# The second matrix product of an attention and MLP kernel, computed for eight of nine blocks with seven half-size products in place of eight

## The chip, the cores and the metric

The kernel runs on one core of a Trainium2 chip. The core has a matrix engine (PE, TensorE; its weight loads are shown apart as PEld), two engines for elementwise work that can read the matrix engine's result memory (DVE, VectorE, and ACT, ScalarE), a third elementwise engine that works between tiles in SBUF alone in this kernel and also issues part of the DMAs (POOL, GpSimd), and an engine that only issues DMAs here (SP, SyncE). Matrix results land in PSUM, which this kernel treats as one tile `pb` of 8 banks of 512 fp32 columns on 128 partitions. The metric is device time of one execution in microseconds; lower is better.

## The reference

Eight batches, eight heads, 576 positions, head size 64. A bias that depends on the distance of two positions alone is added to the scores, and the attention result is the input x (4608 rows by 512) of an MLP:

```python
scores = scale * np.matmul(q, k.transpose(0, 1, 3, 2)) + bias   # bias by distance
attn = softmax(scores)
x = (attn @ v).transpose(0, 2, 1, 3).reshape(4608, 512)
h = x @ w_in                                # 4608 x 2048
g = h + sin(alpha * h) ** 2 / (alpha + 1e-09)
out = g @ w_out                             # 4608 x 512
```

## The kernel before

All matrix operands are fp16, all sums fp32. The MLP's rows are cut into nine blocks of 512 (0 to 8); the attention is done batch by batch, t = 0 to 7. One turn t has two stages. In the *attention stage* PE multiplies k and q for 21 units (16 of kind "A", and C, B and X units for the last 64 positions), each into one or two of the PSUM banks 0 to 5; ACT takes the exponential of each unit into a tile `u`; DVE multiplies by the bias factor (L738, two SBUF operands `u` and `m2r`); PE multiplies by v (`plan_av`), DVE divides by the sums (L952, L953) into `xn`, and a transposing DMA issued on SP writes the result into `xT`. In the *MLP stage* `plan_moe_in` computes block b = t: for each of 16 slices f of 128 hidden columns, four matmuls of `w_in` and `xT` into one bank, sine on ACT (L1068), square on ACT or DVE (L1075, L1077), and DVE writes slice f of the tile `g` (L1082). ACT changes its function table between the stages. Turn 7 does blocks 7 and 8.

The product that is changed is `plan_mo(b, a)`: for each 128 rows a = 0 to 3 of block b, 16 matmuls of 128 x 512 (one for each f; weights are the slice of g, the moving operand is row block f of `w_out`) accumulate in one bank. The tag "mo" may use banks 7 and 6 and so may the attention times v ("av"); in practice one holds a tile of the one and one a tile of the other. DVE or ACT copies the finished bank to `outs` and SP stores it.

The order of all work is not written by hand. `Plan.run` is a list scheduler that runs when the program is built: each piece of work is a `Task` with a cost for every engine that can do it, dependencies, a priority and buffers; the plan emits tasks in the order of its own clock, and each engine's queue then has that fixed order. On the chip an engine takes its queue strictly in order and waits at semaphores that the framework sets for every hazard on a tile. The `plan_mo` matmuls have the lowest priority and are marked `fill`: they go between the other PE work, at most `QUOTA` = 44 of them during an attention stage. So block b's w_out product runs on PE mostly during the attention stage of turn b + 1, and in the tail after turn 7 for blocks 7 and 8.

Three things of the plan matter below. First, work that is emitted inside another task is not costed: when slice 0 of g is written, `gg` also emits, on POOL, a one-element copy that waits for that slice (`tick`), six loads of v and two DMAs that stage k and q for turn b + 2:

```python
if f == 0 and 1 <= b < T - 1:
    nc.gpsimd.tensor_copy(out=tick, in_=gcell[b].v[0:1, 0, 0:1])
    load_v16(b + 1)
    if b + 2 < T:
        stage_kq(b + 2)
```

Second, on SP the loads of the next turn's k and q (`load_kqT`, L396 and L397) stand behind the transposing DMAs of this turn, and POOL's two copies of k's last 64 rows (L402) wait for them and stand ahead of `tick` in POOL's queue. Third, a framework semaphore orders two engines' accesses to the same PSUM bank by the order in which they were emitted.

## Time and profile before

| what | value |
|---|---|
| median of 3 timed runs | 373.82 us (372.97 to 376.73) |
| span of the profiled execution | 374.9 us |
| PE busy | 368.2 us |
| ACT busy | 315.7 us |
| DVE busy | 257.8 us |
| POOL busy | 91.9 us |
| matmuls of g and w_out, 128 x 512 | 560, and 16 each of 384 and 128 columns |

The page of the profile gives no time of the profiled execution besides its span, which runs from the first to the last instruction; it lies 0.3% above the median and within the three runs. "Busy" of PE counts a matmul from start to its modelled end; matmuls are pipelined, so the duration of one (0.379 us for 512 columns) is longer than the step from one start to the next. A line of the timeline merges instructions of one kind that follow each other: start, length of the whole stretch, engine, line, operation, tiles, shape and count, and in brackets the idle time before it and what ended it.

### The profile page before, as it was taken

What the parts mean: (1) busy time and instruction counts of PE and PEld (TensorE: products, weight loads), DVE (VectorE), ACT (ScalarE), POOL (GpSimd) and SP (SyncE); (2) the same over time, 40 slices, a digit from 0 to 9 for tenths busy, and PEclk for the clock granted to TensorE, in tenths of its full rate; (3) what the DMA queues carried; (4) which work ended last, traced back from release to release, by engine and by line L of the source; (5) the groups of instructions that cost most, each with busy time, mean ns of one, the idle gap of its engine ahead of it and who ended that gap; (6) DMA issues with size and microseconds to landing.
All of it is one profiled execution on the core that took longest, in us unless ns stands there. A gap on an engine that the chain in (4) does not pass through costs nothing.

```text
span 374.9 us, 8925 instructions
## 1 busy us (share of the span) xinstructions
PE 368.2 (98%) x3576; PEld 197.4 (53%) x3576; DVE 257.8 (69%) x559; ACT 315.7 (84%) x431; POOL 91.9 (25%) x133
## 2 busy tenths in 40 slices
PE   8999999999999999999999999999999999999996
PEld 3455454644455455684564455444576455444443
DVE  3496976759676967597758867786759675879000
ACT  2787989979997999899989999799979997999211
POOL 7368270037000640055002800090006000000000
PEclk9999999999999999999999999999999999999999
DMA  9969999369922998199917992699249121000112
GB/s 168 201 113 192 200 173 160 83 112 112 133 64 62 151 143 123 48 160 137 133 48 134 125 168 58 122 88 187 59 111 118 65 58 47 7 27 5 73 69 85
DMA packets 149114, 40.49 MB, mean 108 GB/s; under 512 B 137080, under 2 KB 143568, under 8 KB 149072
## 3 DMA queue, kind: packets, MB, share of 16 engines
q0 software_dynamic: 96032, 17.67, 58.3%
q1 hardware_dynamic: 52864, 22.16, 24.6%
q8 instruction: 28, 0.46, 0.5%
q10 hardware_dynamic: 176, 0.09, 0.1%
q14 instruction: 14, 0.11, 0.1%
HBM read 37.73 MB, written 16.56 MB: 145 GB/s over the span
## 4 chain that ended last, share of the span: by engine, by line
PE 95%; ACT 3%; DVE 1%; issue 0%; ACTq 0%
PE pb L457 92%; ACT u L707 3%; PE pb L556 2%; PE pb L1024 1%; PE pb L550 0%; DVE xn L953 0%; DVE u L738 0%; DVE qT L539 0%; DVE zz L508 0%; ACT outs L537 0%; ACT xT L537 0%; DVE rd L952 0%; PE pb L646 0%; PE pb L934 0%; ACTq L537 0%
## 5 line engine op out<-in xcount | busy, mean ns | idle before, releaser
L707 ACT ACTIVATE u<-pb 128x1024 f16<-128x1024 f32 (+1 forms) x146 | 137.4, 1017 | 11.9 <-PE pb L457 10.5
L457 PE MATMUL pb<-w_out,g 128*128 128x512 f16 (+2 forms) x592 | 139.0, 374 | 0.0
L457 PE MATMUL pb<-xT,w_in 128*128 128x512 f16 (+4 forms) x704 | 127.4, 340 | 0.0
L1082 DVE SCALAR_TENSOR_TENSOR g<-sq,inv_a,pb 128x512 f16<-128x512 f16 x144 | 101.3, 744 | 7.1 <-PE pb L457 2.7
L1068 ACT ACTIVATE s<-pb,alphaT 128x512 f16<-128x512 f32 x144 | 92.9, 692 | 12.4 <-PE pb L457 11.9
L457 PEld LDWEIGHTS <-w_in 128*128 128x128 f16 x704 | 64.6, 98 | 57.4
L457 PEld LDWEIGHTS <-g 128*128 128x128 f16 x592 | 53.9, 98 | 60.2 <-issue 5.6
L738 DVE TENSOR_TENSOR u<-u,m2r 128x512 f16<-128x512 f16 (+1 forms) x128 | 62.3, 493 | 33.6 <-ACT u L707 31.9
L457 PEld LDWEIGHTS <-u 128*128 128x128 f16 x1152 | 43.4, 97 | 9.6 <-issue 4.6
L402 POOL COPY kt<-kT 64x256 f16<-64x256 f16 x12 | 4.9, 410 | 172.0 <-DMA kT<-staged_k 107.8
L457 PE MATMUL pb<-qT,kT 64*128 64x64 f16 (+1 forms) x512 | 43.3, 293 | 1.1 <-ACT u L707 0.6
L1075 ACT ACTIVATE sq<-s 128x512 f16<-128x512 f16 x69 | 43.1, 637 | 1.2 <-DVE g L1082 0.3
L457 PE MATMUL pb<-v,u 128*128 128x65 f16 x1024 | 43.7, 193 | 0.0
L1077 DVE TENSOR_TENSOR sq<-s 128x512 f16<-128x512 f16 x75 | 30.9, 422 | 12.5 <-ACT s L1068 11.7
L953 DVE TENSOR_TENSOR xn<-pb,rd 128x256 f16<-128x256 f32 (+2 forms) x59 | 28.5, 483 | 2.0
L457 PEld LDWEIGHTS <-kT 64*128 64x128 f16 x512 | 16.2, 95 | 23.1 <-issue 16.8
L457 PE MATMUL pb<-vh,u 128*128 128x130 f16 x128 | 28.2, 221 | 0.0
L407 POOL DMA_DIRECT2D v<-in_v_dram x28 | 24.8, 900 | 4.0 <-DMA nat<-in_k_dram 2.1
L537 ACT ACTIVATE outs<-pb 128x512 f32<-128x512 f32 (+2 forms) x12 | 6.9, 572 | 19.9 <-PE pb L457 19.9
L952 DVE RECIPROCAL rd<-pb 128x4 f32<-128x4 f32 (+2 forms) x59 | 11.0, 186 | 13.3 <-PE pb L457 13.1
L539 DVE COPY outs<-pb 128x512 f32<-128x512 f32 x25 | 17.2, 686 | 4.1 <-PE pb L457 4.1
L1146 ACT ACT_TABLE_LOAD x15 | 19.2, 1283 | 0.3
(75 smaller groups left out, 192.5 us busy)
## 6 DMA issues: line engine op xcount, KB each, us to landing
out_dram<-outs SPq DMA_DIRECT2D x35, 256.0 KB, 2.8
v<-in_v_dram POOLq DMA_DIRECT2D x28, 128.0 KB, 4.6
staged_k<-in_k_dram POOLq DMA_DIRECT2D x6, 576.0 KB, 8.9
staged_q<-in_q_dram POOLq DMA_DIRECT2D x6, 576.0 KB, 12.1
w_in<-in_moe_w_in_dram POOLq DMA_DIRECT2D x4, 512.0 KB, 8.5
w_out<-in_moe_w_out_dram POOLq DMA_DIRECT2D x4, 512.0 KB, 14.5
w_out<-in_v_dram SPq DMA_DIRECT2D x6, 128.0 KB, 5.7
xT<-xn SPq DMA_TRANSPOSE x47, 2.4
```

The lines of the kernel that those rows point to most:

```text
L407: nc.gpsimd.dma_start(out=vs[t % 2][:, c, :, 0:D], in_=vp[128 * c : 128 * c + 128],)
L457: nc.tensor.matmul(out=out, lhsT=lhsT, rhs=rhs, start=start, stop=stop)
L539: k_of(e).tensor_copy(out=o, in_=i)
L707: nc.scalar.activation(out=o, in_=x, func=AF.Exp, scale=0.125)
L738: nc.vector.tensor_tensor(out=io, in0=io, in1=m2[:, 2 * p : 2 * p + 2, x0 : x0 + hi - lo], op=ALU.mult)
L952: nc.vector.reciprocal(out=r, in_=x[:, :, :, D])
L953: nc.vector.tensor_tensor(out=xn[:, 0:n].rearrange("p c (z d) -> p c z d", z=2), in0=x[:, :, :, 0:D], in1=r.unsqueeze(3).to_broadcast([128 ...
L1068: nc.scalar.activation(out=s16.v, in_=h.v, func=AF.Sin, scale=alphaT[:, f : f + 1])
L1075: nc.scalar.activation(out=sq.v, in_=s16.v, func=AF.Square)
L1077: k_of(e).tensor_tensor(out=sq.v, in0=s16.v, in1=s16.v, op=ALU.mult)
L1082: nc.vector.scalar_tensor_tensor(out=gcell[b].v[:, f, :], in0=sq.v, scalar=inv_a[:, f : f + 1], in1=h.v, op0=ALU.mult, op1=ALU.add,)
L1146: nc.scalar.preload_act_table_set(name)
```

## The change

Blocks 1 to 8 get `plan_mo_w` in place of `plan_mo`; block 0 is as before. The product of one block, g (512 rows by 2048) times w_out (2048 by 512), is cut into 2 by 2: rows 0 to 255 and 256 to 511 of g, columns 0 to 255 and 256 to 511 of w_out, and even and odd slices f of the sum. Strassen's method in Winograd's form makes the four quarters of the result from seven products instead of eight. The products' operands are quarters of g and w_out or sums of them:

- Sums of w_out, once (`plan_wt`): 12 pieces of 128 x 512 into three new tiles `wt`, and four in place, all on POOL.
- Sums of g, for each block: S1 to S4, each in two pieces of 128 x 1024 (four slices by 256), on DVE or POOL as the plan chooses. S3 and S2 go to new tiles `half3` and `half2`, S1 and S4 overwrite quarters of g. In each piece S1 follows S3 and S2 follows S1; S4 follows S2 and product 2.
- Seven products, each 2 x 8 matmuls of 128 x 256: for rows c = 0 and 1 of 128, eight slices f. They all use bank 7, columns 0 to 255 for c = 0 and 256 to 511 for c = 1, and all blocks 1 to 8 hold that bank as one buffer, "mw", so that "av" keeps bank 6 alone.
- After each product and c, 256 columns are taken out of PSUM: a copy (DVE or ACT) after products 1 and 2, an addition with an earlier fp32 result on DVE (tiles `sn`, `outs`) after the other five. Two products accumulate onto the one before them in PSUM, after its value was taken out.
- The result goes out in quarters of 256 x 256, one DMA for both c.

Around it: blocks 2 to 7 let the first two slices' matmuls of `plan_moe_in` start before all of x is there (`SPLIT`), the attention tail of the turn before goes into the second run of units instead of the first (`TAIL_RUN`), the scheduler's window and one priority are larger, and several small tiles of the start share memory with `wt[0]`. The start flag of the `w_in` matmuls is set once per bank.

```diff
-NBUF = {"ut": 2, "u": 2, "g": 2, "s16": 3, "sq": 3, "outs": 5, "xn": 6}
+NBUF = {"ut": 2, "u": 2, "g": 2, "s16": 3, "sq": 3, "outs": 5, "xn": 6, "s2": 1, "s3": 1, "sn": 3}
-BANKS = {"h": (0, 1, 2, 3, 4, 5), "av": (6, 7), "mo": (7, 6)}
+BANKS = {"h": (0, 1, 2, 3, 4, 5), "av": (6, 7), "mo": (7, 6), "mw": (7,)}
-WINDOW = 700
+WINDOW = 900
+T_WT = 50.0
+SG = 4
+TAIL_RUN = 1
-SPLIT = {0: 3, 1: 3}
+SPLIT = {0: 3, 1: 3, **{b: 2 for b in range(2, 8)}}
-AV_PRI = 400
+AV_PRI = 800
...
+    wt = [sgl.tile([128, 8, 256], F16, name=f"wt{i}") for i in range(3)]
+    half = {k: sgl.tile([128, 8, 256], F16, name=f"half{k}") for k in (2, 3)}
...
-            tl = plan_tail(t - 1, base) if i == 0 and t > 1 else None
+            tl = plan_tail(t - 1, base) if i == TAIL_RUN and t > 1 else None
...
+    def plan_wt():
+        w = w_out16.rearrange("p (f z) n -> p z f n", z=2)
...
+            x1 = sub(wt[0][:, fs], b12, b11, [], pri)
+            x3 = sub(wt[2][:, fs], b22, b12, [], pri)
+            x2 = sub(wt[1][:, fs], b22, wt[0][:, fs], [x1], pri)
+            x4 = sub(b12, b21, wt[1][:, fs], [x2, x3] + mo_of[0][2 * j : 2 * j + 4], pri)
...
+    def plan_mo_w(b):
...
+        def s_task(name, j, n, ins, out, op, deps, new, use):
...
+                k_of(e).tensor_tensor(out=o, in0=x, in1=y, op=op)
+            t = plan.add({"DVE": 0.16 + n * 256 * 0.00053, "POOL": 0.15 + n * 256 * 0.0022}, f, deps,
+                         pri0 + j, new=new, use=use)
...
+        def prod(i, k, fresh):
+            lhs, rhs, need, src = prods[k]
+            for c in range(2):
+                cs = slice(256 * c, 256 * c + 256)
+                for f in range(0, 8, 2):
...
+                        for ff in (f, f + 1):
+                            nc.tensor.matmul(
+                                out=mo.v[:, cs], lhsT=lhs(ff, c), rhs=rhs(ff),
+                                start=fresh and ff + c == 0, stop=ff == 7,
+                                skip_group_check=not fresh or c == 1)
+                    t = plan.add({"PE": 2 * t_pe(256)}, mm, chain[0] + need(f) + need(f + 1) + (
+                        ends.get(c, []) if f == 0 else []), 500000000 + 100 * b + i,
...
+        def c_op(k, name, other, c, rows=None, col=None):
...
+                if other is None:
+                    copy_on(e, o, mo.v[:, cs])
+                else:
+                    nc.vector.tensor_tensor(out=o, in0=tiles[other][0].v[:, cs], in1=mo.v[:, cs], op=ALU.add)
...
+        block(0, 1, True, "a", None)
+        block(1, 2, False, "C11", None, 0, 0)
...
+        block(2, 6, True, "x", "a")
+        block(3, 5, True, "y", "x")
+        block(4, 7, True, "C22", "y", 1, 1)
+        block(5, 4, False, "C21", "x", 1, 0)
+        block(6, 3, True, "C12", "y", 0, 1)
...
-            for a in range(4):
-                plan_mo(b, a)
+            if b == 0:
+                for a in range(4):
+                    plan_mo(b, a)
+                plan_wt()
+            else:
+                plan_mo_w(b)
```

## The prediction

> **What bounds the kernel now.** I read the busy shares first, then the chain that ended last, then the granted clock.

> ```profile
> PE 368.2 (98%) x3576; PEld 197.4 (53%) x3576; DVE 257.8 (69%) x559; ACT 315.7 (84%) x431; POOL 91.9 (25%) x133
> ...
> PEclk9999999999999999999999999999999999999999
> ...
> PE 95%; ACT 3%; DVE 1%; issue 0%; ACTq 0%
> ```

> PE is the chain, at full clock and without a hole. Less PE work shortens the kernel one for one, and any wait that PE gets lengthens it one for one; the other engines matter only through such waits. The timeline of PE gives the step of a matmul (start, length, count):

> ```profile
> 1.27 2.32 PE L457 MATMUL pb<-zz 128*128 128x512 f16 x5 [1.27 <-DVE zz L508]
> ...
> 156.81 4.39 PE L457 MATMUL pb<-xT,w_in 128*128 128x320 f16 x39
> ...
> 236.19 5.13 PE L457 MATMUL pb<-xT,w_in 128*128 128x512 f16 x23
> ```

> Last line: one matmul lasts 0.379, so a step is (5.13 - 0.38) / 22 = 0.216 for 512 columns. The middle line alternates 192 and 320 columns, 256 on average: (4.39 - 0.3) / 38 = 0.108; the starts in the trace give 0.0825 and 0.1358, so 0.109 for 256. (The first line, at the program's start, is at 0.42 for 512.) Weight loads hide even behind 65 columns (step 0.029), so behind 256 too; that the smaller matmuls cost more than half is excluded.

> **PE work removed.** A block took 64 x 0.216 = 13.82 and takes 7 x 16 x 0.109 = 12.25: 1.57 less, 12.6 for eight blocks. That is the whole gain.

> **Evacuations.** Prices by shape, and the copy that falls away:

> ```profile
> L953 DVE TENSOR_TENSOR xn<-pb,rd 128x256 f16<-128x256 f32 x29 | 12.3, 425 | 1.0
> L738 DVE TENSOR_TENSOR u<-u,m2r 128x768 f16<-128x768 f16 x64 | 35.9, 563 | 8.4 <-ACT u L707 7.5
> L738 DVE TENSOR_TENSOR u<-u,m2r 128x512 f16<-128x512 f16 x64 | 26.8, 423 | 25.1 <-ACT u L707 24.3
> L539 DVE COPY outs<-pb 128x512 f32<-128x512 f32 x25 | 17.2, 686 | 4.1 <-PE pb L457 4.1
> ```

> An addition of 256 columns out of PSUM is like the first row, 0.43; a copy of 256 about the same (the ACT copy of 256 lasts 0.38). The plan lets PE fill one half of bank 7 while the other is read, and then 0.87 of matmuls would cover each evacuation. But in the built program's order and semaphores the wait is for the whole bank: the matmul of half c = 1 that is next in PE's queue waits until half 0 has been read. Where it stands directly behind the matmul that the evacuation waits for, PE loses the round trip: matmul start to end 0.27, to DVE's start 0.04, evacuation 0.43, back to PE 0.06 (the usual gaps in the trace), less the step 0.11: **0.68**. Going through the queue I find 55 of the 112 evacuations so placed: 3 in block 1's turn, 5 in each of the next five, 4 beside block 8's w_in matmuls and 23 in the tail, where PE has no other work. In the other places 0.8 to 1.7 of score or v work stands between. 55 x 0.68 = **37.4** (33 to 41 for evacuations of 0.35 to 0.5). [...]

> DVE itself gets 80 additions x 0.43 = 34, 26 sums x 0.70 (from 0.563 and 0.423: 0.15 + 0.00054 per element, 1024 elements) = 18, and about 4 less of copies: 258 + 48 = 306. That is no bound by itself. "av" with one bank costs nothing: one of the two banks was always held by a w_out tile. The start flags and shared tiles cost nothing; `SPLIT` and `TAIL_RUN` only reorder PE work.

> **The sums of g on POOL.** From block 2 on POOL's queue has S3, S1, S2 of the first piece, S2 of the second, S4 of the second; DVE has S3, S1 of the second and S4 of the first. Product 6 needs S2. What stands ahead of S3 on POOL (turn 4), and DVE's last two g slices:

> ```profile
> 203.79 0.83 POOL L402 COPY kt<-kT 64x256 f16<-64x256 f16 x2 [30.36 <-PE pb L457]
> 204.68 0.26 POOL L1087 COPY tick<-g 1x1 f16<-1x1 f16 x1
> 204.89 3.54 POOL L407 DMA_DIRECT2D v<-in_v_dram  x4
> 208.39 1.29 POOL L426 DMA_DIRECT2D vh<-in_v_dram  x2
> 209.62 2.29 POOL L390 DMA_DIRECT2D staged_k<-in_k_dram  x1
> 211.32 2.80 POOL L390 DMA_DIRECT2D staged_q<-in_q_dram  x1
> ...
> 211.33 1.40 DVE L1082 SCALAR_TENSOR_TENSOR g<-sq,inv_a,pb 128x512 f16<-128x512 f16 x2
> ```

> The plan's clock knows nothing of these DMA issues; POOL is free only at 214.1, after all of g is written (212.7). It becomes later: next turn's k load stands on SP behind the store of C21. In before it is issued at 197.8, 2.0 after the first w_in matmul (195.8). Now ahead of it are 2.5 of PE work (12 w_in matmuls, 4 of product 4, 3 transposes, 18 of v), 0.6 to evacuate, a store issue (0.5) and a transposing DMA (1.2): 5.0. The stage's end moves by 1.2 of that, so POOL's adds start 1.7 later, at **215.8**.

> A POOL addition of 1024 elements is in no row. The nearest are POOL's additions of 128 (the timeline again):

> ```profile
> 20.12 0.76 POOL L724 TENSOR_TENSOR u<-u,mhr 128x128 f16<-128x128 f16 x1
> 20.84 0.50 POOL L633 COPY tick<-m2r 1x1 f16<-1x1 f16 x1
> 25.32 0.42 POOL L724 TENSOR_TENSOR u<-u,mhr 128x128 f16<-128x128 f16 x1 [0.61 <-ACT u L707]
> ...
> 20.05 1.25 DVE L738 TENSOR_TENSOR u<-u,m2r 128x768 f16<-128x768 f16 x2
> ```

> The undisturbed one (25.32) takes 0.41 for 128 elements. With a fixed part of 0.18 (an undisturbed tick) 1024 take 2.0; with none, 3.25. I take 2.3, near the lower end since every POOL row has a fixed part, and 0.05 between two. [...]

> Product 6's second half is due in block 4's turn at 218.0: it stands behind the seventh score unit, which waits for ACT's fourth exponential (212.95 + 3.77), then 0.3 and eight matmuls. Two exposed evacuations ahead of it make that 219.4. Four additions from 215.8 end at 225.2: **5.8 lost** per block if POOL runs undisturbed.

> It does not. In the fence above POOL's addition at 20.12 takes 0.76 instead of 0.41 while DVE's multiplication of two SBUF tiles runs, and the second of DVE's two waits in turn (1.25 for 0.42 + 0.56). Tick copies take 0.18 alone and 0.26 to 0.50 beside such a DVE instruction; beside DVE instructions with one SBUF tile nothing is stretched. So whichever of the two starts first holds the other off to its end. I walk block 4's queues with that. DVE's S3, S1: 214.6 to 216.0. POOL S3 216.0 to 218.3. DVE's first multiplication to 218.7. POOL S1 to 221.0. DVE's second to 221.6. POOL S2 to 223.9. DVE S4 (which waits for that S2, with C11's second evacuation queued behind it) to 224.6. POOL S2 to 226.9. DVE's third to 227.5, C11's evacuation to 228.1, PE 228.2. Without these waits PE would be there at 219.4 + 0.44 + 0.68 = 220.5: **7.7 lost**, for blocks 2 to 5 30.8. The same walk for block 1 (POOL free at 91.1, g complete at 94.3, one addition of w_out between): 4.5; for block 6 (no staging, 289.4 against 291.9): 4.6. The 12 sums of w_out in turn 1 (1.2 each) meet DVE's multiplications: 0 to 10; I take 4, since 12 meetings cost half a sum each, 7, and DVE is idle a third of the time. That sums to **43.9**.

> Sum on the profiled execution: 374.9 - 12.6 + 37.4 + 43.9 = 443.6. The median of the runs lies 1.1 below the span: **442.5**.

> **Rivals.**
> *No conflict between POOL and DVE*: long POOL additions leave room for DVE. Then 5.8 x 4 + 2.2 + 0.2 = 25.6 in place of 43.9: 424. For it: no POOL instruction over 0.76 of this kind is in the trace. Against it: all the stretched rows. [...]
> *The clock falls*: PE would stand still for about 5 before product 6. If it comes back at the start's 0.42 step for some 3, six turns lose 1.5 to 3 each: 458. For it: the first PE line; against: nothing shows it, since after the start no hole of PE in before is over 0.72. [...]
> *Evacuations alone*: POOL is early enough (its queue reached earlier, additions short): 399.
> *Faster*: the bank wait comes without a cost, since PE's other half really runs under it, and POOL is in time. Then only the 12.6 is left: 361. It decides at 0.15 per exposed evacuation; against it stand the semaphores as built, and 23 of them in a tail without cover.

> **Chances.** Conflict 0.50 (442), none 0.27 (424), clock 0.12 (458), evacuations alone 0.07 (399), faster 0.04 (361). POOL's addition at 2.0 or 3.25 moves the first by -7 or +23. Leaving out the last two and half of the clock's tail: 410 to 466. Faster by over 1% 0.04, within 1% (what a measurement can tell) 0.01, slower 0.95.

> **What would show it.** Matmuls of 256 at a step of 0.109 and 896 of them; DVE additions near 0.43; in PE's waits, `pb` on DVE `sn` and `outs` about 55 times with 0.7 each, and on POOL `half2` with 4 to 7 in each turn; the tail after the last w_in matmul 14 longer; POOL additions over 2.3 stretched beside DVE's. I am wrong if PE hardly waits for DVE in the tail, or if POOL has S2 ready when PE comes.

## The result and the profile after

The changed kernel takes 457.23 us (median of four runs, 456.58 to 457.93) where the kernel before, run beside it, takes 373.39 us. The ratio is 1.224, with a 95% interval of 1.218 to 1.230. The change costs 83.8 us; the forecast was 68.7 us (442.5). All times below are microseconds.

The page of the changed kernel, lines that answer to those shown of before (busy time of each engine, granted clock in 40 slices, chain that ended last):

```profile
PE 375.6 (82%) x3944; PEld 235.9 (52%) x3944; DVE 358.9 (79%) x666; ACT 312.2 (68%) x429; POOL 197.7 (43%) x187
...
PEclk9999999979999699986999799985999999999999
...
PE 50%; DVE 27%; POOL 7%; issue 6%; DMA 6%; ACT 3%; DVEq 0%; ACTq 0%; POOLq 0%; SPq 0%
```

PE was 98% busy and 95% of the chain. It is now 82% busy and half of the chain, and DVE is 27% of the chain where it was 1%. Two more things are new: the clock row has dips in the middle, and DVE's busy time has grown from 257.8 to 358.9, 53 more than the 306 forecast. The trace's record of the granted clock has PE at half speed for 51.3: five stretches (from 96, 151, 202, 257 and 305) and 3.5 at the very end.

Where DVE's time went is in the costliest groups by line, DVE first, then POOL:

```profile
L751 DVE TENSOR_TENSOR u<-u,m2r 128x512 f16<-128x512 f16 (+1 forms) x128 | 94.0, 755 | 9.2 <-ACT u L720 8.0 <-DMA m2r<-e_dram 1.1
L1094 DVE TENSOR_TENSOR sq<-s 128x512 f16<-128x512 f16 x73 | 42.3, 586 | 5.8 <-ACT s L1085 5.7
L1289 DVE TENSOR_TENSOR outs<-sn,pb 128x256 f32<-128x256 f32 x48 | 20.1, 419 | 23.7 <-PE pb L1261 23.5
...
L1204 POOL TENSOR_TENSOR half<-g 128x1024 f16<-128x1024 f16 x21 | 51.3, 2452 | 35.4 <-DVE g L1099 25.1 <-PE pb L1261 7.1 <-DVE g L1204 2.7
```

The same two groups in the kernel before:

```profile
L738 DVE TENSOR_TENSOR u<-u,m2r 128x512 f16<-128x512 f16 (+1 forms) x128 | 62.3, 493 | 33.6 <-ACT u L707 31.9
L1077 DVE TENSOR_TENSOR sq<-s 128x512 f16<-128x512 f16 x75 | 30.9, 422 | 12.5 <-ACT s L1068 11.7
```

The multiplication by the bias factor (L751, two SBUF operands; L738 before) took 493 ns on average and now takes 755. The square (L1094, two SBUF operands; L1077 before) went from 422 to 586 ns. The additions that read PSUM (L1289) take 0.42, as forecast. One POOL addition of 1024 elements takes 2.45 on average; undisturbed ones take 2.12.

PE's waits for the evacuations (the views of before had no such line):

```profile
PE pb L1261 <- DVE outs L552: 27.6, 13, 4.3
PE pb L1261 <- DVE outs L1289: 19.2, 30, 2.8
PE pb L1261 <- DVE sn L1289: 7.7, 14, 1.0
PE pb L1261 <- DVE sn L552: 5.2, 2, 2.7
PE pb L1261 <- DVE g L1099: 4.1, 1, 4.1
...
PE pb L1261 <- ACT sn L550: 1.9, 4, 0.5
PE pb L1261 <- ACT outs L550: 1.9, 3, 0.9
```

A row gives who waited for whom, then the total, the number of waits and the longest. L1289 is an addition out of PSUM, L552 a copy on DVE and L550 one on ACT. Two kinds stand here. The additions make PE wait often, mostly some 0.5 to 0.6 at a time (the longest wait is 2.8). The copies on DVE are few, 15, but take 32.8 in all, up to 4.3 each. The wait of 4.1 is for the last slices of block 1's g. The timeline around two of these pauses, in block 3's w_out product, DVE first, then POOL, then PE (start, length, and in brackets the idle time and what ended it):

```profile
196.44 5.44 DVE L751 TENSOR_TENSOR u<-u,m2r 128x512 f16<-128x512 f16 x2
201.81 0.17 DVE L967 RECIPROCAL rd<-pb 128x4 f32<-128x4 f32 x1
202.01 0.42 DVE L968 TENSOR_TENSOR xn<-pb,rd 128x256 f16<-128x256 f32 x1
202.35 0.41 DVE L552 COPY outs<-pb 128x256 f32<-128x256 f32 x1
203.89 2.59 DVE L1204 TENSOR_TENSOR g<-g,half 128x1024 f16<-128x1024 f16 x1 [1.12 <-POOL half L1204]
206.41 2.46 DVE L751 TENSOR_TENSOR u<-u,m2r 128x768 f16<-128x768 f16 x1
208.79 0.41 DVE L552 COPY outs<-pb 128x256 f32<-128x256 f32 x1
...
195.98 3.23 POOL L1204 TENSOR_TENSOR half<-g 128x1024 f16<-128x1024 f16 x1
199.28 2.19 POOL L1204 TENSOR_TENSOR g<-g 128x1024 f16<-128x1024 f16 x1
201.55 4.39 POOL L1204 TENSOR_TENSOR half<-g 128x1024 f16<-128x1024 f16 x2
206.01 2.44 POOL L1204 TENSOR_TENSOR g<-g,half 128x1024 f16<-128x1024 f16 x1
...
202.82 1.01 PE L1261 MATMUL pb<-w_out,g 128*128 128x256 f16 x4 [3.46 <-DVE outs L552]
203.91 1.03 PE L1261 MATMUL pb<-wt,half 128*128 128x256 f16 x4
209.26 1.01 PE L1261 MATMUL pb<-wt,half 128*128 128x256 f16 x4 [4.31 <-DVE outs L552]
```

The copies of C11 (`outs`, L552) at 202.35 and 208.79 themselves take 0.41. PE waits 3.46 and 4.31 for them, because DVE takes its queue in order and stands ahead of them in two-operand instructions: two multiplications that take 5.44, where the rows of before give 0.42 and 0.56 (the second is of 768 columns; a merged line names the shape of its first), and end just behind POOL's second addition (201.47); then a sum of 2.59 (0.69 where POOL is still) beside POOL's next; then a multiplication of 2.46 (0.56 before). The normalization at 202.01, which reads PSUM, takes its usual 0.42 while POOL adds. The wait for block 1's g is of the same kind: two squares (0.42 each in the row of before) take 4.20 from 92.20 on, beside POOL's additions from 90.61 and 93.93, and PE stands still from 93.64 to 97.77.

The stages: from block 1's first w_in matmul to block 2's and so on to block 6's it takes 48.5, 51.5, 51.6, 51.3 and 53.1 (before: 42.0, 39.3, 39.7, 39.6, 39.6). The tail behind the start of the last w_in matmul is 44.5 instead of 30.3. Lengths of stages are compared here and not their starts: executions of the kernel before differ by some 4 (372.65 to 376.73), and in the profiled one (376.73) the full clock is on record from 20.9, in the changed kernel's from 4.2.

### The profile page after: what moved, and what is told of

It is laid out like the page before. It is cut to its first block, busy times and chain, and to the rows that moved or that the text cites. A ratio compares the mean times of both kernels' runs of the same rounds, so it can differ in the third digit from the quotient of the medians.

```text
span 456.2 us, 9806 instructions
## 1 busy us (share of the span) xinstructions
PE 375.6 (82%) x3944; PEld 235.9 (52%) x3944; DVE 358.9 (79%) x666; ACT 312.2 (68%) x429; POOL 197.7 (43%) x187
## 4 chain that ended last, share of the span: by engine, by line
PE 50%; DVE 27%; POOL 7%; issue 6%; DMA 6%; ACT 3%; DVEq 0%; ACTq 0%; POOLq 0%; SPq 0%
PE pb L1261 20%; PE pb L470 16%; PE pb L1078 14%; DVE u L751 8%; DVE g L1099 4%; DMA w_out<-in_moe_w_out_dram 4%; DVE sq L1094 3%; DVE g L1204 3%; DVE outs L1289 3%; POOL half L1204 2%; ACT s L1085 1%; DVE sn L1289 1%; DVE outs L552 1%; POOL staged_k L403 1%; POOL staged_q L403 1%
## 5 line engine op out<-in xcount | busy, mean ns | idle before, releaser
L1261 PE MATMUL pb<-w_out,g 128*128 128x256 f16 x512 | 72.3, 279 | 44.8 <-DVE outs L1289 18.2
L751 DVE TENSOR_TENSOR u<-u,m2r 128x512 f16<-128x512 f16 (+1 forms) x128 | 94.0, 755 | 9.2 <-ACT u L720 8.0
L1261 PEld LDWEIGHTS <-g 128*128 128x128 f16 x640 | 60.9, 99 | 76.6 <-issue 61.4
L1204 POOL TENSOR_TENSOR half<-g 128x1024 f16<-128x1024 f16 x21 | 51.3, 2452 | 35.4 <-DVE g L1099 25.1
L1261 PE MATMUL pb<-wt,half 128*128 128x256 f16 x256 | 41.4, 300 | 17.9 <-DVE outs L552 13.7
L470 PEld LDWEIGHTS <-u 128*128 128x128 f16 x1152 | 46.4, 99 | 10.4 <-issue 8.2
L1094 DVE TENSOR_TENSOR sq<-s 128x512 f16<-128x512 f16 x73 | 42.3, 586 | 5.8 <-ACT s L1085 5.7
L1092 ACT ACTIVATE sq<-s 128x512 f16<-128x512 f16 x71 | 44.3, 630 | 0.4
L1261 PEld LDWEIGHTS <-half 128*128 128x128 f16 x256 | 25.5, 105 | 27.9 <-issue 19.3
L1289 DVE TENSOR_TENSOR outs<-sn,pb 128x256 f32<-128x256 f32 x48 | 20.1, 419 | 23.7 <-PE pb L1261 23.5
L1204 POOL TENSOR_TENSOR g<-g,half 128x1024 f16<-128x1024 f16 x8 | 18.2, 2275 | 31.7 <-PE pb L1261 31.4
L420 POOL DMA_DIRECT2D v<-in_v_dram x28 | 25.1, 903 | 4.9 <-DMA nat<-in_k_dram 2.5
## 6 DMA issues: line engine op xcount, KB each, us to landing
staged_q<-in_q_dram POOLq DMA_DIRECT2D x6, 576.0 KB, 11.7
```

Of the source, the lines that this page charges most:

```text
L470: nc.tensor.matmul(out=out, lhsT=lhsT, rhs=rhs, start=start, stop=stop)
L751: nc.vector.tensor_tensor(out=io, in0=io, in1=m2[:, 2 * p : 2 * p + 2, x0 : x0 + hi - lo], op=ALU.mult)
L1092: nc.scalar.activation(out=sq.v, in_=s16.v, func=AF.Square)
L1094: k_of(e).tensor_tensor(out=sq.v, in0=s16.v, in1=s16.v, op=ALU.mult)
L1204: k_of(e).tensor_tensor(out=o, in0=x, in1=y, op=op)
L1261: nc.tensor.matmul(out=mo.v[:, cs], lhsT=lhs(ff, c), rhs=rhs(ff), start=fresh and ff + c == 0, stop=ff == 7, skip_group_check=not fresh or ...
```

## The experiments

Theory A: POOL's additions hold up DVE's instructions with two SBUF operands, and the copies behind these, for which PE waits. Theory B: PE and the engine that evacuates take turns on one PSUM bank, 0.68 for each exposed evacuation. Theory C: the products wait because POOL comes late to the sums. Theory F: the fall of the clock is a price of its own.

### All sums of g on VectorE

```diff
-            t = plan.add({"DVE": 0.16 + n * 256 * 0.00053, "POOL": 0.15 + n * 256 * 0.0022}, f, deps,
+            t = plan.add({"DVE": 0.16 + n * 256 * 0.00053}, f, deps,
```

> All 64 sums of g on VectorE (29 of them were GpSimd's in the changed kernel, 457.2 us, among them nearly all of blocks 1 to 6). Theory A, VectorE's fp16 operations with two SBUF inputs stand still while GpSimd adds: VectorE's two-input mask operations fall from a mean of 755 ns back to about 500, its busy time from 359 to some 330 although it makes 29 x 0.69 = 20 us of sums more, the TensorE waits of 2 to 4 us behind a VectorE copy of a result tile are gone (about 30 us of them), the granted clock stays at 1 and its 20 us come back too: 400 to 415 us. Theory B, the time is lost because TensorE and VectorE take turns on one PSUM bank (55 waits of 0.68 us) and because VectorE has too much to do: the 20 us of sums more on VectorE cost rather than save, 450 to 475. Theory C, GpSimd only comes to its sums too late, behind its DMA issues: product 6 is released by VectorE about 5 us earlier in each of five turns: about 430, with mask operations still at 750 ns.

Measured: 413.79, 43.4 less than the changed kernel; ratio to before 1.109 (1.105 to 1.114). POOL made 38 of the 64 sums in the changed kernel, not the 29 that the expectation says, so DVE, which made 26, has 38 more to make. DVE's groups by line:

```profile
L751 DVE TENSOR_TENSOR u<-u,m2r 128x512 f16<-128x512 f16 (+1 forms) x128 | 66.3, 551 | 4.3 <-ACT u L720 3.2 <-DMA m2r<-e_dram 1.0
L1094 DVE TENSOR_TENSOR sq<-s 128x512 f16<-128x512 f16 x64 | 27.5, 437 | 9.5 <-ACT s L1085 9.1
L1204 DVE TENSOR_TENSOR half<-g 128x1024 f16<-128x1024 f16 x32 | 21.3, 683 | 0.0
```

The multiplications are back to 551 ns (theory A had about 500; the 11 that still take over 0.8 all stand between 52.0 and 68.2, beside POOL's sums of w_out), the squares to 437, and DVE's busy time fell from 358.9 to 321.7 although it makes more sums, each in 0.68. The same place in block 3's product, DVE's timeline:

```profile
184.21 0.68 DVE L1204 TENSOR_TENSOR half<-g 128x1024 f16<-128x1024 f16 x1
185.31 0.42 DVE L552 COPY outs<-pb 128x256 f32<-128x256 f32 x1 [0.41 <-PE pb L1261]
185.65 0.68 DVE L1204 TENSOR_TENSOR g<-g,half 128x1024 f16<-128x1024 f16 x1
186.25 1.02 DVE L751 TENSOR_TENSOR u<-u,m2r 128x768 f16<-128x768 f16 x2
188.16 0.43 DVE L552 COPY outs<-pb 128x256 f32<-128x256 f32 x1 [0.89 <-PE pb L1261]
```

The copies of C11 now stand behind sums of 0.68 and multiplications of 0.5, and DVE waits for PE instead of PE for DVE. PE's waits for copies on DVE fall from 32.8 to 5.6, and half speed from 51.3 to 4.8. Theory A has it; B alone would have given a longer time, and C alone about 430.

### No sums of g

```diff
-                k_of(e).tensor_tensor(out=o, in0=x, in1=y, op=op)
-            t = plan.add({"DVE": 0.16 + n * 256 * 0.00053, "POOL": 0.15 + n * 256 * 0.0022}, f, deps,
+                pass
+            t = plan.add({"POOL": 0.01}, f, deps,
...
-            6: (H(s2), lambda f: wt[1][:, f], lambda f: [made[("S2", f)], wdone[f][6]], b2),
+            6: (L(0, 1), lambda f: wt[1][:, f], lambda f: [made[("S2", f)], wdone[f][6]], b2),
```

> The sums of g are left out: products 3, 5, 6 and 7 are taken with the raw quarters of g, so the output is not the reference's; the products, the evacuations and the sums of w_out stay. What is left above the kernel before is the price of the evacuations and of the w_out sums, less 12.6 us of TensorE work. The prediction's own terms give 373.8 - 12.6 + 37.4 + (0 to 10) = 399 to 408, with the granted clock at 1 except in the tail. If the waits between the bank's halves are hidden by other TensorE work more often than was counted: 365 to 385. If the clock falls even so, because the evacuations alone make TensorE pause: 420 or more.

Measured: 409.92, ratio 1.099 (1.097 to 1.101), just above the band from the prediction's terms (399 to 408), with the clock at half for only 3.4, at the very end. So the sums themselves cost 3.9 net when DVE makes them (413.8 against 409.9); the plan, which counts them as 0.01 here, also orders its tasks a little differently. PE's waits for evacuations in this kernel (here L1287 is the addition):

```profile
PE pb L1259 <- DVE outs L1287: 18.0, 35, 0.5
PE pb L1259 <- DVE sn L1287: 7.3, 14, 0.6
...
PE pb L1259 <- DVE outs L552: 3.1, 6, 0.5
PE pb L1259 <- ACT outs L550: 2.8, 5, 0.9
PE pb L1259 <- ACT sn L550: 1.9, 4, 0.5
```

That is 64 waits and 33.1: 5 in block 1's turn, 6 in each of the next five, 3 beside block 8's w_in matmuls and 26 in the tail. The prediction counted 3, 5, 4 and 23, 55 in all.

### The sums made, but not used

```diff
-            6: (H(s2), lambda f: wt[1][:, f], lambda f: [made[("S2", f)], wdone[f][6]], b2),
+            6: (L(0, 1), lambda f: wt[1][:, f], lambda f: raw(0)(f) + [wdone[f][6]], gb),
...
-            x = s_task("S1", j, n, lambda fs=fs: (A(0, 1, fs), A(1, 1, fs)), lambda fs=fs: A(0, 1, fs),
-                       ALU.add, [x], [], [gb])
+            x = s_task("S1", j, n, lambda fs=fs: (A(0, 1, fs), A(1, 1, fs)), lambda fs=fs: s3[:, fs],
+                       ALU.add, [x], [], [gb, b3])
```

In the same way products 5, 7 and 3 take raw quarters, and S4 goes into `half2`.

> The sums of g are made as in the changed kernel and by the same engines, but into tiles that nothing reads: products 3, 5, 6 and 7 take raw quarters of g (the output is not the reference's), so TensorE waits for no sum. Theory A (the sums on GpSimd hold up VectorE's two-input operations, and the copies queued behind them, for which TensorE waits): little is gained, 440 to 458, mask operations still at about 750 ns, TensorE still pausing 2 to 4 us for VectorE's copies. Theory C (the products wait for late sums): the time falls to that of the kernel without sums, about 400.

Measured: 466.43, ratio 1.251 (1.245 to 1.257). No product waits for a sum, and yet it is 56.5 longer than without sums and 9.2 longer than the changed kernel, above theory A's band (440 to 458) too. PE's longest group of waits and DVE's multiplications are those of the changed kernel:

```profile
PE pb L1261 <- DVE outs L552: 34.7, 13, 4.6
```

```profile
L751 DVE TENSOR_TENSOR u<-u,m2r 128x512 f16<-128x512 f16 (+1 forms) x128 | 93.4, 751 | 10.5 <-ACT u L720 9.1 <-DMA m2r<-e_dram 1.5
```

Theory C falls: what costs is that POOL adds at all while DVE works. Why this kernel is 9.2 longer than the changed one stays open; it has two more sums on POOL, and half speed for 61.4 instead of 51.3.

### Two PSUM banks in the last two blocks

```diff
+T2 = 7
...
+    slot2 = Buf("av"), Cell()
...
+                    two = b >= T2 and c == 1
...
+                        mv = slot2[1] if two else mo
...
-                                out=mo.v[:, cs], lhsT=lhs(ff, c), rhs=rhs(ff),
-                                start=fresh and ff + c == 0, stop=ff == 7,
+                                out=mv.v[:, cs], lhsT=lhs(ff, c), rhs=rhs(ff),
+                                start=fresh and ff + (0 if two else c) == 0, stop=ff == 7,
```

> As the changed kernel, but in blocks 7 and 8 (beside block 8's w_in product and in the tail) the upper half of the products goes to a second PSUM bank, which is free there. Theory B (a half's copy orders everything on its bank: TensorE waits for VectorE and back): the 23 exposed waits of the tail and the 4 beside block 8 go, 0.68 us each: the stretch behind the last w_in product falls from 44.3 to about 29 us, all in all 16 to 18 us less, 439 to 442. If instead VectorE's own work in the tail (copies and additions, 28 x 0.42 us, and the sums of g) sets its length: under 5 us less, 452 or more.

Measured: 441.42, ratio 1.185 (1.181 to 1.189), 15.8 less than the changed kernel. The tail falls from 44.5 to 30.1. Theory B's forecast holds (the tail was to be 29).

### No turns on the bank in any block

```diff
+    fake = half[2].rearrange("p f n -> p (f n)")[:, 0:1024].bitcast(F32)
-                    copy_on(e, o, mo.v[:, cs])
+                    copy_on(e, o, fake[:, cs])
-                    nc.vector.tensor_tensor(out=o, in0=tiles[other][0].v[:, cs], in1=mo.v[:, cs], op=ALU.add)
+                    nc.vector.tensor_tensor(out=o, in0=tiles[other][0].v[:, cs], in1=fake[:, cs], op=ALU.add)
```

> The run without sums of g (409.9 us), with one thing more left out: the copies and additions that evacuate the products read a tile of zeros in SBUF instead of the PSUM bank (the output is not the reference's), so that TensorE and they no longer take turns on that bank; they stay in number, size, engine and order. Theory B for all blocks: the 64 waits of TensorE for them, 0.52 us each and 33.1 us in all, go, and the time falls to 373 to 379, with turns of about 38.5 us and a tail of 28 to 29. Rival H (TensorE would wait there for something else, above all for ScalarE's exponentials, once these waits are gone): most of what is won in turns 2 to 7 is lost again, 385 to 395, and only the tail falls by its 14 to 16 us.

Measured: 366.09, ratio to before 0.981 (0.979 to 0.983), and 43.8 less than the kernel without sums, which differs only in what the evacuations read. The edit takes away the waits in both directions: PE no longer waits for the evacuations, nor they for the products. Busy times of the page:

```profile
PE 352.4 (97%) x3944; PEld 231.0 (63%) x3944; DVE 292.6 (80%) x639; ACT 311.7 (85%) x430; POOL 113.8 (31%) x150
```

PE is at 97% again, with DVE as busy as in the kernel without sums (292.6 and 290.1). Nothing takes the place of the 64 waits (the turns are 38.2, the tail is 24.7), so rival H falls. The time is even below theory B's band, because that counted only the idle 33.1. A wait costs more than its idle time: besides 0.52 idle, PE loses the time from a matmul's start to its end beyond a step, 0.27 - 0.11 = 0.16 by the prediction's numbers. 64 x 0.68 = 43.5; measured 43.8. PE's own times agree: between the two spans (408.3 and 365.1) its idle time falls by 34.2 and its busy time by 9.0.

### The plan's constants alone

```diff
-WINDOW = 700
+WINDOW = 900
+TAIL_RUN = 1
-SPLIT = {0: 3, 1: 3}
+SPLIT = {0: 3, 1: 3, **{b: 2 for b in range(2, 8)}}
-AV_PRI = 400
+AV_PRI = 800
-            tl = plan_tail(t - 1, base) if i == 0 and t > 1 else None
+            tl = plan_tail(t - 1, base) if i == TAIL_RUN and t > 1 else None
```

> The kernel before with nothing of Strassen's method, only with the changed kernel's constants of the plan (window 900, split w_in matmuls in blocks 2 to 7, priority 800 of the probability product, the last rows' step one run later). In the changed kernel block 0's w_in stage starts 4.4 us earlier than in the kernel before and block 1's at the same time. Theory D, the plan's constants win these 4 us and the sums of w_out in turn 1 lose them again: here block 1's w_in stage starts near 70.5 us instead of 74.8, and the whole takes 367 to 371. Theory E, turn 1's start is set by the arrival of w_out from memory, so that what turn 0 gains waits there in either kernel: block 1's stage starts at 74 to 75.5 and the time is 371 to 376. If the constants harm the turns behind, above 377.

The kernel also has the changed kernel's start flags of the `w_in` matmuls.

Measured: 377.69, ratio 1.012 (1.005 to 1.018); its four runs lie between 375.55 and 379.52. This is neither theory's time, but above 377, the third case. Block 1's stage does begin at 70.7, but the early start that both theories set out from is no work of the constants: it comes and goes between executions (the last section), and the kernel with both edits below, which has the same constants, begins its block 0 stage at 32.5. What can be read is the length from block 0's first w_in matmul to block 1's: 42.3 here, 42.3 in the kernel before and 46.7 in the changed one. Up to there the changed kernel differs from this one in the sums of w_out on POOL and in small tiles that share memory. The two kernels of the last experiment below, which share these tiles but make the sums of w_out in turn 3, take 42.9 and 43.4, so the sums cost 3.3 to 4.4. Each later turn is 1.1 to 2.2 shorter here than before, but the w_out matmuls that were put off come back: the two parts of the last w_in stage stand 11.9 apart, where before it is 1.9. The constants win nothing.

### Matmuls that keep TensorE busy

```diff
                 if other is None:
                     copy_on(e, o, mo.v[:, cs])
+                    if name == "C11" and 2 <= b <= 6 and e == "DVE":
...
+                        for _ in range(20):
+                            warm1(k, 256)
```

> As the changed kernel, but behind each copy of C11 that VectorE makes in blocks 2 to 6 (ten places) TensorE has 20 matmuls of 256 columns to do whose result nothing uses (2.2 us at full clock), so that it works on while that copy is held up. In the changed kernel the granted clock is at a half for 51.3 us, and TensorE is busy in 30.0 of these: at full clock that is 15 us less. Theory F (the pauses of TensorE bring the clock down, and this alone costs 10 to 15 us): half-speed time below 20 us, and 442 to 448 us in all, though there is more work. If the clock falls for another reason, or its fall lies beside VectorE's waits and costs nothing: 455 to 475.

Measured: 459.59 (the median of its three runs from 458.33 to 461.54; a fourth took 467.3), ratio 1.230 (1.222 to 1.238), half speed for 34.0. The time is in the second band, but half speed fell only part of the way, and the unused matmuls themselves waited 13.4 for normalizations on DVE, so that it tells neither theory. It was done with more of them, in other banks:

> As the run before that kept TensorE busy, but with 30 unused matmuls of 256 columns (3.3 us) behind each copy of a first product and of C11 that VectorE makes in blocks 2 to 6, and into banks of the scores, because in that run ten pauses only moved to the unused matmuls themselves, which waited 13.4 us for VectorE's normalization to leave its bank; 34.0 us of half speed were left of 51.3. Theory F (the half speed is itself a price of 10 to 15 us): half speed below 20 us, and 442 to 450 us. Theory G (VectorE, held up by GpSimd's sums, sets the length of these turns, and TensorE's slower matmuls lie beside its waits): the half speed goes as far, but the time stays at 455 to 470.

Measured: 483.98, ratio 1.295 (1.287 to 1.302), outside both bands. The page:

```profile
PE 431.7 (89%) x4544; PEld 290.6 (60%) x4544; DVE 349.2 (72%) x666; ACT 312.7 (65%) x429; POOL 196.8 (41%) x187
...
PEclk9999999979999999999999999899998999999999
```

The clock stays up throughout turns 4 and 5 and is at half for 21.0 in all, but 600 matmuls of 0.109 are 65 more of work, and 26.8 of it stands beyond the pauses. With work for PE in the pauses half speed went from 51.3 to 34.0 and 21.0; the two runs don't tell what the fall of the clock costs the changed kernel.

### Both edits that helped

This kernel has the edits of the first and of the fourth experiment together.

> Both edits that helped, together: all sums of g on VectorE (413.8 us alone) and two PSUM banks for the halves in blocks 7 and 8 (15.8 us less alone). If they act in different places, as theories A and B have it, the gains add: 396 to 399 us, with a tail of about 28 us behind the last w_in product. If VectorE, which now has all sums to make, sets the length of the tail, the second edit is worth less: 403 to 411.

Measured: 394.89, ratio 1.058 (1.052 to 1.065): 18.9 less than with the sums on DVE alone, so the two gains add, and a little more (just below the band). The tail is 26.9, 3.4 shorter than in the kernel before. This is the hint for the next two.

### Strassen's method in the last blocks only

```diff
+T2 = FIRST = 7
+WT_TURN = 3
-            if b == 0:
+            if b < FIRST:
                 for a in range(4):
                     plan_mo(b, a)
-                plan_wt()
             else:
                 plan_mo_w(b)
+            if b == WT_TURN:
+                plan_wt()
```

These lines are against the changed kernel. The constants of the plan are those of the kernel before, all sums are on DVE, and in the second kernel `FIRST` and `T2` are 8.

> The kernel before, with its constants, and Strassen's method in blocks 7 and 8 alone: all sums on VectorE (those of w_out too, in turn 3, 16 of 512 elements), halves in two PSUM banks. From the run with both edits: its tail behind the last w_in product is 26.9 us where the kernel before has 30.3, its stage from block 7's first w_in matmul to the last 32.8 where that has 30.0; together 0.7 us less. TensorE's work falls by 2 x 1.57 = 3.1 us. If the sums of w_out (about 6 us of VectorE in small pieces) hide in turn 3, the time is 1 to 3 us below the kernel before: 370 to 373. If VectorE is too full for them, or product 6 waits for the sums of g: 374 to 378.

> The same with Strassen's method in block 8 alone: 1.57 us of TensorE work less, and only one set of sums of g, made after block 8's last g while block 7's product keeps TensorE busy. If these sums are hidden, 0.5 to 1.5 us below the kernel before (372 to 373); if the last products wait for them or for their copies at the very end (seven stores instead of four), level or up to 2 us above it.

Measured: blocks 7 and 8 370.53, ratio to before 0.9931 (0.9904 to 0.9958); block 8 alone 371.87, ratio 0.9976 (0.9938 to 1.0015). The first is faster than the kernel before, by 2.5. Its page, busy times and chain:

```profile
PE 365.1 (98%) x3656; PEld 206.1 (55%) x3656; DVE 279.7 (75%) x608; ACT 315.1 (85%) x433; POOL 92.1 (25%) x133
...
PE 93%; ACT 4%; DVE 2%; issue 1%; ACTq 0%
```

PE has 3.1 less to do and stays at 98%, as in the kernel before: two blocks' worth of the saving, with all that cost the other blocks left out. That block 8 alone is faster is not shown: its interval includes 1.

## Why the prediction was right, and where it was not

The runs make a chain, in which each step from the second on changes one thing in the work (the plan's order of tasks can change a little with it; the medians of before lie between 373.0 and 373.5 in the comparisons; 373.2 is taken):

| step | measured | forecast |
|---|---|---|
| before (373.2) to no sums of g, no turns on the bank (366.1): TensorE's work, sums of w_out, the rest | -7.1 | -12.6 + 4 = -8.6 |
| turns on the bank (to 409.9) | +43.8 | +37.4 |
| sums of g, made on DVE (to 413.8) | +3.9 | |
| 38 of these on POOL (to 457.2) | +43.4 | |
| the last two together | +47.3 | 43.9 - 4 = +39.9 |

The forecasts of the three rows add up to 68.7, the measured steps to 84.0.

**TensorE's work.** The step of a 256-column matmul is 0.109 in the trace, and the saving is there once nothing else stands in its way: -12.6, 3.3 to 4.4 for the sums of w_out and 1.1 to 2.2 unexplained make the -7.1.

**Sums of w_out in turn 1.** Forecast 4 (0 to 10), measured 3.3 to 4.4. All kernels with these sums in turn 1 take 46.0 to 47.7 from block 0's first w_in matmul to block 1's, the four without 42.3 to 43.4.

**Evacuations.** The mechanism and the price of 0.68 held (43.8 / 64). The step that failed is the count: "Going through the queue I find 55 of the 112 evacuations so placed". In the run without sums 64 places waited, two more in block 1's turn, one more in each of the next five, three more in the tail and one fewer beside block 8's w_in matmuls. The same view of the changed kernel has 66. This is 6.4 of the 15.3 by which the sum of the rows fell short.

**The sums of g on POOL.** That POOL and DVE hold each other up was forecast from a few stretched rows of 0.76 and 1.25, and it carries the result: without POOL's additions 43.4 is gone. (The POOL rows of `u` and `mhr` that the prediction calls additions are multiplications by the bias factor; its price of 2.3 for an addition of 1024 was near the 2.12 measured without disturbance.) The trace shows it: two multiplications that take 0.42 and 0.56 in the rows of before take 5.44 beside POOL's additions, and a copy out of PSUM takes 0.41 in the same stretch. The step that failed is what PE waits for. The signature named was PE waiting "on POOL `half2` with 4 to 7 in each turn"; all such waits together are 4.4. The run with unused sums shows that no product needs to wait for a sum for the time to be lost. PE waits for C11's copy, which the walk of block 4's queues had at its end ("with C11's second evacuation queued behind it") but for one pause only; the trace has two or three in each product of blocks 2 to 5, since C11's first copy, and in two places a copy of product 1, are held up as well. In block 1's turn the one long pause, 4.13, is for g, behind squares that were held up. The rival without a conflict (424) is out.

**The clock.** The condition of that rival came true: PE paused for 2.7 to 4.3 and the granted clock fell to a half with it, in five turns. The prediction gave this chance 0.12 and no place in its sum. The rival's "some 3" at the slow step was not shown: the five stretches at half speed last 6.83 to 13.65. Between the changed kernel and the one with all sums on DVE, span less PE's busy time differs by 33.1 and PE's busy time, for the same 3944 matmuls, by 11.7. So of the 44.8 between the two spans at most some 12 is matmuls at half clock. The chain that ended last in the changed kernel bears on whether this time is really lost. Its pieces around the end of the second pause shown above (start, length, what):

```profile
206.48 2.39 DVE u L751
208.87 0.35 DVE outs L552
209.22 0.04 issue
209.26 1.86 PE pb L1261 x8
211.12 2.40 PE pb L470 x32
```

Here the half clock lasts to 212.41, so 3.15 of PE's work on the chain is at half clock. In the five stretches together it is 23.1, which at full clock would be half of that. The estimate from this one chain is thus 11.6 for the fall of the clock; no run held the clock up and left all else as it was, and the two runs with unused matmuls could not tell.

This makes part of the last row luck. Against the kernel without sums, PE's idle time grew by 33.7 and its busy time by 14.2. The forecast for this row was 39.9, all of it pauses. The pauses came out some 6 smaller than that, and the matmuls at half clock, which the sum had left out, made up for it and more. That the rival's 458 is nearest to the measured 457.2 is no sign that its terms were right, since 6.4 of the excess over 442.5 is the count of evacuations.

**What was costed at nothing.** "`SPLIT` and `TAIL_RUN` only reorder PE work": with the other two constants they cost the old kernel 4.2 (1.9 to 6.8), of which late starts can be a part. In the changed one there is room for at most the unexplained 1.1 to 2.2.

## What to carry to other kernels

An operation moved to an engine that looks idle is not free when it holds up a busy engine, as GpSimd's additions do here with VectorE's instructions of two SBUF operands: count these in that stretch, and price each at up to the whole length of the other engine's instruction (here 2.46 for 0.56), with everything queued behind it. When a large product is split into smaller ones, each piece brings an evacuation; where the next matmul in TensorE's queue writes the same PSUM bank, TensorE loses a round trip, here 0.68 in 64 places against the 1.57 that a whole block's seven products save. A change that loses over the whole kernel may still win where its costs are absent: in the last two blocks, with free banks and the sums on DVE, it is worth 2.5.

## What the runs showed of the hardware

The length of a pause alone does not decide in this trace. With its time cut into stretches of 3.41 that begin where the falls begin, PE was busy, by the profile's modelled ends, for 0.16 to 0.33 of the stretch just ahead of each fall (0.29 ahead of the half speed at the very end), and for 0.47 or more of each of the 112 others at full clock. The pauses at 142, 251 and 350 lie across a border of two such stretches, in which PE was busy for 0.47 to 0.75.

At the program's start the full clock comes at different times in different executions: the record has it from 4.2 in the changed kernel's profiled execution and from 20.9 in that of the kernel before. (The clock row of a page shows nines there too, since it counts time without a record as full.) The matmuls agree: at the start of the kernel before an unused one of 256 columns takes 0.39 up to 19.08 and 0.28 from 21.45 on. In the kernel with the plan's constants alone one takes 0.39 at 6.11 and 0.28 at 8.48, in the kernel with both edits 0.39 still at 16.35. Block 0's w_in stage begins at 32.5 in the kernel before and at 28.1 in the changed one. The two late executions are some 4 longer than the others of their kernel: that of the kernel before takes 376.7, where the three beside it take 372.6 to 373.8, and that of the kernel with both edits 398.6, where the other three take 394.6 to 395.1. By the modelled ends PE was busy for 0.74 of the first 3.41 with work in the kernel before, and for 0.86 of the 3.41 ahead of the rise in the changed one. Why the former then stays slow through 17.1 in which PE is busy for 0.89 to 1.0 of each 3.41 stays open. These 4 are more than the 2.5 that separate the best kernel from the one before, so those two are compared over 12 and 23 executions.
